# Seven operations per piece of weights, a scale from magnitudes, a convolution planned to end ahead of its transform, and four halves on another engine

## The chip, the cores and the metric

The kernel runs on one core of a Trainium2 chip. A core has a matrix engine (TensorE, PE in the profile), a vector engine (VectorE, DVE), an activation engine (ScalarE, ACT), a general engine (GpSimd, POOL) and a queue for transfers (SyncE, SP). Each works through its own list of instructions in order, and waits on semaphores for the others. The metric is the time of one execution on the device in microseconds (us); the kernel before has a median of 1158.82 us over three runs (1158.05 to 1159.72).

## The reference

Eight batches of 4224 rows with 192 columns go through four steps. The two weight matrices arrive as 64-bit floats, two 32-bit words each.

```python
w = np.exp(weight_gen - max(weight_gen, axis=-1)); w = w / (sum(w) + 1e-09)    # [8, 4224, 8 heads, 7 taps]
x = einsum('bshk,bskhg->bshg', w, windows_of_7_rows(x))      # dynamic convolution, 24 columns to a head
u = x + real(fft(fft(x, axis=1), axis=2))                    # over 4224 rows, then 192 columns
un = (u - mean(u)) / sqrt(var(u) + 1e-06)
out = u + maximum(un @ w_ch1, 0.0) @ w_ch2                   # 192 -> 768 -> 192
```

## The kernel before, in words

**Layout.** 4224 rows are 128 partitions times 33 rows. A batch is worked in nine groups: eight of four rows (128 x 768 elements) and one of a single row. Names carry batch and group: `u_3_0` is batch 3, group 0; in `conv` the first group of a batch is group 0 and the last, of one row, is group 8.

**Convolution** (`conv`, L296). For each group DVE multiplies the rows of `x_sb` by the seven taps (L405; the first product goes into the group's sum `u`, the six others into `pr`, five buffers), and POOL adds them up (L414). Batches 0 and 1 share the sums out otherwise in part. POOL then folds the sum (`sm`, L428), PE makes the first stage of the row transform of it (`pg`, L435), ACT and DVE put that into `gt` (L440 to L446), and SP writes `gt` to a scratch array `g_d` in DRAM (L449). The taps of a batch come from `softmax_taps` (L261): DVE takes the maximum (L273) and subtracts it (L274), ACT the exponential (L276), DVE the sum (L278), the small constant (L279) and the reciprocal (L280), and each group multiplies its own taps by it (L362). From batch 2 on this is one piece of 1848 elements for a batch, and `next_conv` issues it behind the last product of the batch before.

**Transform** (`transform`, L460). SP reads `g_d` back in another order (`g`, L471), PE does the second stage (`pp`, L481), ACT copies it to `pq`. For the first matmul of it the whole convolution of the batch must have gone through `gt`, the write and the read.

**Mix and norm** (`mix`, L502; `norm`, L528). PE does the column transform (`eo`, L510), DVE adds it to `u` (L516 to L525). The norm takes mean and variance on DVE (`bn`, first three groups of batch 0 and first two of batch 1) or on ACT, normalises on ACT (`un`, L565), casts to fp16 (`hl`, L573), and subtracts that from `un` for a second fp16 half in two instructions of 512 and 256 elements (L574, L576). These two are on DVE where `quick` holds, which is for the five groups named, and on POOL elsewhere. SP transposes `hl` into `ht` (L582).

**MLP** (`mlp`, L587). A group has six tiles: PE does the first layer (`ph`, L607, fp16 high and low halves of the weights), ACT takes the positive part into `hh` (L617), DVE its low half (L618), PE the second layer (`po`, L630), DVE scales and adds to `u` (L635), SP writes the group out.

**Weights** (`prep_w1`, `prep_w2`, `split_w2`). The first matrix is unpacked in three pieces before the first MLP, the second in three pieces around it. `words_to_f32` (L194) makes a 32-bit float of the two words of each element in eight DVE instructions of 384 elements, L200 to L212. `weight_scale` (L169) finds a power of two: for each of three pieces it masks the exponent (L176) and takes the maximum (L177), then the maximum over pieces and partitions. `split_f32` makes the fp16 halves, high on ACT (L217), low on DVE (L218).

**Order.** The program is issued as streams, each with a start and an end in units of an MLP group: `add(start, end, gen)`, and `run` takes the stream that is due next. For batch b >= 2, with t0 = 9 b, the transform goes from t0 - 4.4 (`PP_AT`) to t0 - 3.0, and the convolution from `free_at`, where the transform of the batch before was due, to t0 - 4.4. Batch 1 has numbers of its own, and the MLP of batch 0's group 7 is in part held behind its transform. A scheduler then sets the order of each engine from dependencies and its own estimate of durations, so a small change of these numbers moves rows on every engine.

Of the kernel before, what the change touches and what calls it, by code (L numbers as in the profile page):

```python
# [10 lines left out]
F16 = mybir.dt.float16  # L11
F32 = mybir.dt.float32
I32 = mybir.dt.int32
AF = mybir.ActivationFunctionType
ALU = mybir.AluOpType
AX = mybir.AxisListType
# [14 lines left out]
EARLY = 7.4  # L31
HELD = 7.0
SPLIT = 4
PP_AT = 4.4
MIX_STEP = 0.8
PE_SUMS = {(0, 0), (0, 1), (0, 3), (0, 5), (0, 7)}
POOL_TAPS = {(0, 0): (5, 6), (0, 1): (5, 6), (0, 3): (6,), (1, 0): range(7), (1, 1): range(7)}
# [51 lines left out]
def tile_dynconv_fnet_mlp(  # L89
# [76 lines left out]
    def temp(nm, dt):  # L166
        return sb.tile([P, PW], dt, tag="hh", name=nm, bufs=10)

    def weight_scale(words, bits, nm):  # L169

        mask, unit, least, up, down = {32: (0x7F800000, 1.0, 4.0 * 2 ** 23, 257.0, -3.0),
                                       64: (0x7FF00000, 8.0, 900.0 * 2 ** 20, 1153.0, -899.0)}[bits]
        mx = cpool.tile([P, len(words)], F32, name=f"mx_{nm}")
        for i, word in enumerate(words):
            ex = temp(f"ex_{nm}{i}", I32)
            nc.vector.tensor_scalar(out=ex, in0=word, scalar1=mask, scalar2=None, op0=ALU.bitwise_and)  # L176
            nc.vector.tensor_reduce(out=mx[:, i:i + 1], in_=ex, axis=AX.X, op=ALU.max)  # L177
        m1 = cpool.tile([P, 1], F32, name=f"m1_{nm}")
        nc.vector.tensor_reduce(out=m1, in_=mx, axis=AX.X, op=ALU.max)
        m2 = cpool.tile([P, 1], F32, name=f"m2_{nm}")  # L180
        row = pst("ph", 3, [P, P], F32, f"mr_{nm}")
        nc.tensor.matmul(row[0:1, :], lhsT=m1, rhs=ident32, start=True, stop=True)
        nc.vector.tensor_reduce(out=m2[0:1], in_=row[0:1, :], axis=AX.X, op=ALU.max)
        every = pst("ph", 3, [P, 1], F32, f"me_{nm}")
        nc.tensor.matmul(every, lhsT=ones, rhs=m2[0:1], start=True, stop=True)
        nc.vector.tensor_scalar_max(out=m2, in0=every, scalar1=least)
        sc = cpool.tile([P, 2], I32, name=f"sc_{nm}")
        nc.vector.tensor_scalar(out=sc[:, 0:1], in0=m2, scalar1=-unit, scalar2=up * 2 ** 23,
                                op0=ALU.mult, op1=ALU.add)
        nc.vector.tensor_scalar(out=sc[:, 1:2], in0=m2, scalar1=unit, scalar2=down * 2 ** 23,  # L190
                                op0=ALU.mult, op1=ALU.add)
        return sc.bitcast(F32)

    def words_to_f32(raw, out, nm, bank):  # L194

        hi, lo = raw[:, :, 1], raw[:, :, 0]
        v = nc.vector
        a, w = [pst(*bank, [P, PW], dt, f"{x}_{nm}") for x, dt in (("pa", I32), ("pw", F32))]
        t = temp(f"t_{nm}", I32)
        v.tensor_scalar(out=a, in0=hi, scalar1=3, scalar2=0x3FFFFFFF,  # L200
                        op0=ALU.logical_shift_left, op1=ALU.bitwise_and)
        v.scalar_tensor_tensor(out=t, in0=hi, scalar=-0x40000000, in1=a, op0=ALU.bitwise_and, op1=ALU.bitwise_or)
        v.tensor_scalar(out=a, in0=hi, scalar1=0x7FF00000, scalar2=None, op0=ALU.bitwise_and)
        v.scalar_tensor_tensor(out=w, in0=a, scalar=float(0x38100000), in1=t.bitcast(F32),
                               op0=ALU.is_ge, op1=ALU.mult)
        v.tensor_scalar(out=t, in0=w.bitcast(I32), scalar1=23, scalar2=23,
                        op0=ALU.logical_shift_right, op1=ALU.logical_shift_left)
        v.tensor_scalar(out=a, in0=lo, scalar1=3, scalar2=None, op0=ALU.logical_shift_right)
        r = t.bitcast(F32)
        v.scalar_tensor_tensor(out=r, in0=a, scalar=2.0 ** -49, in1=r, op0=ALU.mult, op1=ALU.mult)  # L210
        out = w if out is None else out
        last_word.append(v.tensor_tensor(out=out, in0=w, in1=r, op=ALU.add))  # L212
        return out
# [314 lines left out]
    def norm(b, g):  # L528

        T = min(4, N2 - 4 * g)  # L530
        u = uv = us[b, g]
        st = sb.tile([P, 4, 2], F32, tag="st", name=f"st_{b}_{g}", bufs=2)
        rs = sb.tile([P, 3, 4], F32, tag="rs", name=f"rs_{b}_{g}", bufs=2)
        junk = sb.tile([P, D], F16, tag="junk", name=f"junk_{b}_{g}", bufs=2)
        quick = NG * b + g < QUICK or (b == 1 and g < 2)
        if NG * b + g < QUICK:
            halves = [pst("ph", 3, [P, 2, D], F32, f"un_{b}_{g}_{i}") for i in range(2)]
        else:
            un = sb.tile([P, 4, D], F32, tag="un", name=f"un_{b}_{g}", bufs=1)
            halves = [un[:, 0:2], un[:, 2:4]]  # L540
        if quick:
            bn = sb.tile([P, 4, 6], F32, tag="bn", name=f"bn_{b}_{g}", bufs=2)
            for t in range(T):
                nc.vector.bn_stats(out=bn[:, t, :], in_=uv[:, t, :])
                last_bn[b, g] = nc.vector.bn_aggr(out=st[:, t, :], in_=bn[:, t, :])
            nc.scalar.activation(rs[:, 0, 0:T], st[:, 0:T, 1], AF.Sqrt, bias=eps_t)
            neg = -1.0
        else:
            for t in range(T):
                nc.scalar.activation(junk, uv[:, t, :], AF.Identity, accum_out=st[:, t, 0:1])  # L550
            neg = -1.0 / D
            nc.scalar.mul(rs[:, 2, 0:T], st[:, 0:T, 0], neg)
            for t in range(T):
                nc.scalar.activation(junk, uv[:, t, :], AF.Square, bias=rs[:, 2, t:t + 1],  # L554
                                     accum_out=st[:, t, 1:2])
            nc.scalar.activation(rs[:, 0, 0:T], st[:, 0:T, 1], AF.Sqrt, bias=eps_t, scale=1.0 / D)
        nc.vector.reciprocal(out=rs[:, 0, 0:T], in_=rs[:, 0, 0:T])
        if quick or b == 0:
            for t in range(T):
                nc.vector.tensor_scalar(out=rs[:, 1, t:t + 1], in0=st[:, t, 0:1], scalar1=rs[:, 0, t:t + 1],  # L560
                                        scalar2=neg, op0=ALU.mult, op1=ALU.mult)
        else:
            nc.gpsimd.tensor_tensor(out=rs[:, 1, 0:T], in0=rs[:, 2, 0:T], in1=rs[:, 0, 0:T], op=ALU.mult)  # L563
        for t in range(T):
            nc.scalar.activation(halves[t // 2][:, t % 2, :], uv[:, t, :], AF.Identity,  # L565
                                 bias=rs[:, 1, t:t + 1], scale=rs[:, 0, t:t + 1])
        yield 0.5
        warm = NG * b + g == 0
        hl = sb.tile([P, 4, 2 * D], F16, tag="hl", name=f"hl_{b}_{g}", bufs=2)
        lo_eng = nc.vector if quick else nc.gpsimd  # L570
        spans = [(un, 0, T)] if NG * b + g >= QUICK else [(h, 2 * i, 2 * i + 2) for i, h in enumerate(halves)]
        for src, t0, t1 in spans:
            nc.scalar.copy(hl[:, t0:t1, 0:D], src[:, 0:t1 - t0, :])  # L573
            lo_eng.tensor_tensor(out=hl[:, t0:t1, 2 * P:3 * P], in0=src[:, 0:t1 - t0, 0:P],  # L574
                                 in1=hl[:, t0:t1, 0:P], op=ALU.subtract)
            last_lo[NG * b + g] = lo_eng.tensor_tensor(out=hl[:, t0:t1, D:2 * P], in0=src[:, 0:t1 - t0, P:D],  # L576
                                                       in1=hl[:, t0:t1, P:D], op=ALU.subtract)
        if warm:
            keep_warm(("ph", 3), f"hl{g}", hl[:, 0, 0:P], hl[:, T - 1, 0:2 * D], WARM[2])
        hls[NG * b + g] = hl  # L580
        ht = sb.tile([P, 4, 3, P], F16, tag="ht", name=f"ht_{b}_{g}", bufs=3)
        nc.sync.dma_start(ht[:, 0:T].rearrange("p t q m -> p (t q) m"),  # L582
                          hl[:, 0:T, :].rearrange("p t d -> p (t d)"), transpose=True)
        state[b, g] = (us.pop((b, g)), ht)
        yield 2.0
# [148 lines left out]
    for b in range(B):  # L734
        t0 = NG * b
        pp_at, mix_at, step = (NG - HELD + 0.6, NG - HELD, 0.6) if b == 1 else (PP_AT, 3.0, MIX_STEP)
        if b > 0:
            add(free_at, t0 - pp_at, next_conv(b) if b > 1 else rest())
            add(t0 - pp_at, t0 - mix_at, transform(b))
            free_at = t0 - pp_at  # L740
        for g in range(NG):
            if b > 0 or g >= QUICK:
                at = t0 - mix_at + step * g + (0.7 if b == 0 else 0)
                add(at, at + step, late_mix(g) if b == 0 and g >= QUICK else mix(b, g))
                add(max(at + step, t0 + g - 2.0), t0 + g - 1.0, norm(b, g))
# [38 lines left out]
```

## Time and profile before

| what | value |
|---|---|
| median of three runs | 1158.82 us |
| the profiled execution | 1160.23 us, of which 1158.5 us are the span from the first to the last instruction; 1.73 us lie around it |
| mean granted PE clock | 0.982 |
| busy: PE, DVE, POOL, ACT | 1085.7, 987.3, 873.7, 776.9 us |
| first MLP matmul | at 129.89 us |
| first matmul of the transforms of batches 1 to 7 | 234.72, 360.78, 485.65, 611.49, 738.97, 866.21, 992.99 us |

Times in the trace count from the start of the span. A row of the timeline shows start, duration, engine, line, operation, output and input, how many instructions the row joins, and in square brackets how long the engine was idle before it and what it waited for. The starts of the transforms of successive batches lie 124.87, 125.84, 127.48, 127.24 and 126.78 us apart from batch 2 on. After the last transform has begun 165.5 us are left.

### The profile page before, as it was taken

How to read it: one execution, taken by the hardware profiler on the slowest of the kernel's cores; microseconds unless marked ns; L12 is line 12 of the kernel's file. 1: busy time of each engine (PE TensorE's matmuls, PEld its weight loads, DVE VectorE, ACT ScalarE, POOL GpSimd, SP SyncE). 2: the span in 40 equal slices, each digit the busy share in tenths (PEclk: the TensorE clock that was granted, in tenths of full speed). 3: DMA queues.
4: the chain of work that ended last, by engine and by line, in shares of the span. 5: the costliest groups of instructions: out<-in, count | busy, mean ns of one | idle time of the engine just before them, and what ended most of it. 6: DMA issues, size and time to landing. Idle time of an engine off the chain costs nothing. (4 is left out here: it accounts for less than half of the span.)

```text
span 1158.5 us, 23681 instructions
## 1 busy us (share of the span) xinstructions
PE 1085.7 (94%) x8476; PEld 819.0 (71%) x8476; DVE 987.3 (85%) x1830; ACT 776.9 (67%) x2360; POOL 873.7 (75%) x747
## 2 busy tenths in 40 slices
PE   5787699998799999999999999999999999999998
PEld 3346388776577777678777877778767867777777
DVE  7998998889989998999989998899988997356443
ACT  1014587453896589648985699668974798579832
POOL 5948699699896999699978999599959999011200
PEclk9997799999999999999999999999999999999999
DMA  8325233622474147513564247514652243412321
GB/s 307 118 92 152 41 99 104 183 79 64 122 194 126 52 117 197 142 56 110 131 178 110 59 121 204 137 53 117 160 128 65 56 91 79 126 34 68 83 45 46
DMA packets 156502, 128.72 MB, mean 111 GB/s; under 512 B 108571, under 2 KB 133088, under 8 KB 156384
## 3 DMA queue, kind: packets, MB, share of 16 engines
q1 hardware_dynamic: 156384, 127.21, 40.6%
q8 instruction: 67, 1.10, 0.4%
q14 instruction: 51, 0.42, 0.1%
HBM read 61.46 MB, written 39.37 MB: 87 GB/s over the span
## 5 line engine op out<-in xcount | busy, mean ns | idle before, releaser
L414 POOL TENSOR_TENSOR u<-u,pr 128x768 f32<-128x768 f32 (+1 forms) x395 | 655.7, 1679 | 67.4 <-DVE pr L405 51.5
L630 PEld LDWEIGHTS <-hh 128*128 128x128 f16 x4248 | 364.6, 98 | 81.8 <-DVE hh L618 5.9
L630 PE MATMUL po<-w2h,hh 128*128 128x192 f16 x2832 | 416.2, 246 | 5.6 <-DVE hh L618 4.3
L607 PE MATMUL ph<-ht,w1h 128*128 128x512 f16 (+1 forms) x1296 | 396.2, 363 | 5.9 <-DMA ht<-hl 2.9
L405 DVE TENSOR_TENSOR pr<-x_sb,wp 128x768 f32<-128x768 f32 (+1 forms) x420 | 357.3, 873 | 13.1 <-POOL u L414 10.2
L630 PE MATMUL po<-w2l,hh 128*128 128x192 f16 x1416 | 346.4, 246 | 0.0
L618 DVE SCALAR_TENSOR_TENSOR hh<-ph,hh 128x512 f16<-128x512 f32 (+1 forms) x390 | 244.8, 632 | 110.9 <-ACT hh L617 109.4
L607 PE MATMUL ph<-ht,w1l 128*128 128x512 f16 (+1 forms) x864 | 310.8, 363 | 0.0
L617 ACT ACTIVATE hh<-ph 128x512 f16<-128x512 f32 (+1 forms) x390 | 213.8, 551 | 137.9 <-PE ph L607 110.3
L607 PEld LDWEIGHTS <-w1h 128*128 128x128 f16 x1296 | 125.8, 99 | 92.3 <-issue 2.0
L565 ACT ACTIVATE un<-u,rs 128x192 f32<-128x192 f32 x264 | 123.9, 536 | 23.1 <-POOL rs L563 9.8
L607 PEld LDWEIGHTS <-w1l 128*128 128x128 f16 x864 | 85.1, 98 | 53.9 <-issue 6.6
L574 POOL TENSOR_TENSOR hl<-un,hl 128x512 f16<-128x512 f32 (+1 forms) x67 | 71.8, 1071 | 67.2 <-issue 29.7
L554 ACT ACTIVATE junk<-u,rs 128x192 f16<-128x192 f32 x244 | 110.7, 454 | 3.8
L550 ACT ACTIVATE junk<-u 128x192 f16<-128x192 f32 x244 | 88.1, 361 | 15.6 <-DVE u L520 12.8
L510 PE MATMUL eo<-cs_sb,pq 97*128 97x97 f32 x544 | 82.5, 276 | 5.3 <-DVE u L520 3.7
L485 ACT COPY pq<-pp 97x204 f32<-97x204 f32 (+1 forms) x96 | 46.9, 489 | 55.9 <-PE pp L481 55.8
L510 PEld LDWEIGHTS eo<-cs_sb,pq 97*128 97x128 f32 x544 | 75.2, 193 | 9.9 <-issue 6.7
L635 DVE SCALAR_TENSOR_TENSOR u<-po,isc,u 128x384 f32<-128x384 f32 (+1 forms) x122 | 72.3, 592 | 5.0 <-PE po L630 4.9
L410 PE MATMUL pa<-pr,ident 128*128 128x384 f32 x140 | 53.2, 520 | 21.0 <-POOL pr L403 11.8
L428 POOL TENSOR_TENSOR sm<-u 128x382 f32<-128x382 f32 x64 | 65.5, 1023 | 9.1 <-ACT u L423 8.7
L563 POOL TENSOR_TENSOR rs<-rs 128x4 f32<-128x4 f32 (+1 forms) x61 | 12.1, 200 | 68.3 <-ACT hh L617 38.8
(106 smaller groups left out, 1306.7 us busy)
## 6 DMA issues: line engine op xcount, KB each, us to landing
out_dram<-u SPq DMA_DIRECT2D x64, 384.0 KB
x_sb<-in_x_dram SPq DMA_DIRECT2D x48, 384.0 KB
g<-g_d SPq DMA_DIRECT2D x40, 336.0 KB
x_sb<-in_x_dram SPq DMA_DIRECT2D x8, 864.0 KB
g_d<-gt SPq DMA_DIRECT2D x32, 195.0 KB
g_d<-gt SPq DMA_DIRECT2D x32, 189.0 KB
w<-in_weight_gen_dram SPq DMA_DIRECT2D x6, 924.0 KB
x_sb<-in_x_dram SPq DMA_DIRECT2D x8, 672.0 KB
```

What stands on the lines that cost most here:

```text
L405: last_product[b] = nc.vector.tensor_tensor(out=dst, in0=rows, in1=wk, op=ALU.mult)
L414: adder.tensor_tensor(out=u, in0=u, in1=pr, op=ALU.add)
L510: nc.tensor.matmul(eo[:, e, j, :], lhsT=pq[0:DH, e, r, r:r + P], rhs=cs_sb[:, e, :], start=True, stop=True)
L550: nc.scalar.activation(junk, uv[:, t, :], AF.Identity, accum_out=st[:, t, 0:1])
L554: nc.scalar.activation(junk, uv[:, t, :], AF.Square, bias=rs[:, 2, t:t + 1], accum_out=st[:, t, 1:2])
L565: nc.scalar.activation(halves[t // 2][:, t % 2, :], uv[:, t, :], AF.Identity, bias=rs[:, 1, t:t + 1], scale=rs[:, 0, t:t + 1])
L574: lo_eng.tensor_tensor(out=hl[:, t0:t1, 2 * P:3 * P], in0=src[:, 0:t1 - t0, 0:P], in1=hl[:, t0:t1, 0:P], op=ALU.subtract)
L607: last_ph[n] = nc.tensor.matmul(ph[:, 0:T], lhsT=wt[:, cs_], rhs=ht[:, 0:T, blk], start=(i == 0), stop=(i == len(terms) - 1))
L617: nc.scalar.activation(a[:, 0:T], ph[:, 0:T], AF.Relu)
L618: nc.vector.scalar_tensor_tensor(out=l[:, 0:T], in0=ph[:, 0:T], scalar=0.0, in1=a[:, 0:T], op0=ALU.max, op1=ALU.subtract)
L630: nc.tensor.matmul(po[t // 2][:, t % 2, :], lhsT=hx[:, t], rhs=wx[:, c2, :], start=(c2 == 0 and i == 0), stop=(c2 == NH - 1 and i == len(t ...
L635: nc.vector.scalar_tensor_tensor(out=lt, in0=po[t // 2][:, 0:t % 2 + 1], scalar=scales[0][:, 1:2] if f32 else isc, in1=lt, op0=ALU.mult, o ...
```

## The change

Four things change. `words_to_f32` loses the shift of the lower word (old L208): the lower word is read as an unsigned number straight from the raw words, with a factor of 2 to the power -52 where it was -49, and the exponent goes to `a`, where `t` held it before. `weight_scale` takes the maximum of the magnitude of each piece, read as 32-bit float, and masks the exponent once, of the three maxima. `PP_AT` goes from 4.4 to 4.2 and a new `CONV_LEAD` of 0.2 is taken off the end of a convolution: for batches 2 to 7 the convolution still ends at t0 - 4.4, the transform begins at t0 - 4.2, and the next convolution is due to begin at t0 - 4.2. And the low halves of the first two groups of batch 1 go from DVE to POOL; those of batch 0's first three groups stay on DVE.

```diff
-PP_AT = 4.4
+CONV_LEAD = 0.2
+PP_AT = 4.2
...
         for i, word in enumerate(words):
-            ex = temp(f"ex_{nm}{i}", I32)
-            nc.vector.tensor_scalar(out=ex, in0=word, scalar1=mask, scalar2=None, op0=ALU.bitwise_and)
-            nc.vector.tensor_reduce(out=mx[:, i:i + 1], in_=ex, axis=AX.X, op=ALU.max)
+            nc.vector.tensor_reduce(out=mx[:, i:i + 1], in_=word.bitcast(F32), axis=AX.X, op=ALU.max, apply_absolute_value=True)
+        ex = cpool.tile([P, len(words)], I32, name=f"ex_{nm}")
+        nc.vector.tensor_scalar(out=ex, in0=mx.bitcast(I32), scalar1=mask, scalar2=None, op0=ALU.bitwise_and)
         m1 = cpool.tile([P, 1], F32, name=f"m1_{nm}")
-        nc.vector.tensor_reduce(out=m1, in_=mx, axis=AX.X, op=ALU.max)
+        nc.vector.tensor_reduce(out=m1, in_=ex, axis=AX.X, op=ALU.max)
...
-        v.tensor_scalar(out=t, in0=w.bitcast(I32), scalar1=23, scalar2=23,
+        v.tensor_scalar(out=a, in0=w.bitcast(I32), scalar1=23, scalar2=23,
                         op0=ALU.logical_shift_right, op1=ALU.logical_shift_left)
-        v.tensor_scalar(out=a, in0=lo, scalar1=3, scalar2=None, op0=ALU.logical_shift_right)
         r = t.bitcast(F32)
-        v.scalar_tensor_tensor(out=r, in0=a, scalar=2.0 ** -49, in1=r, op0=ALU.mult, op1=ALU.mult)
+        v.scalar_tensor_tensor(out=r, in0=lo.bitcast(U32), scalar=2.0 ** -52, in1=a.bitcast(F32), op0=ALU.mult, op1=ALU.mult)
...
-        lo_eng = nc.vector if quick else nc.gpsimd
+        lo_eng = nc.vector if NG * b + g < QUICK else nc.gpsimd
...
-            add(free_at, t0 - pp_at, next_conv(b) if b > 1 else rest())
+            add(free_at, t0 - pp_at - (CONV_LEAD if b > 1 else 0), next_conv(b) if b > 1 else rest())
             add(t0 - pp_at, t0 - mix_at, transform(b))
```

The change moves rows on all engines. Three places follow; line numbers of the kernel after are two higher than those of before up to `words_to_f32` and one higher behind it.

DVE at the start of batch 3's convolution, before (`wp_3` its taps, `hh_1_4_3` the low half of MLP tile 3 of batch 1's group 4):

```order
L280 RECIPROCAL wp_3_3463<-wp_3_3463 128x264
L444 TENSOR_TENSOR gt_2_8_3448<-pg_2_8_3446,up_2_8_3450 128x95
L446 TENSOR_TENSOR gt_2_8_3448<-pg_2_8_3446,up_2_8_3450 128x95
L618 SCALAR_TENSOR_TENSOR hh_1_4_2_3400<-ph_1_4_2_3388,hh_1_4_2_3400 128x512
L635 SCALAR_TENSOR_TENSOR u_1_3_1337<-po_1_3_0_3305,isc_88,u_1_3_1337 128x384
L362 TENSOR_TENSOR wp_3_3463<-w_3_3464,wp_3_3463 128x224
L618 SCALAR_TENSOR_TENSOR hh_1_4_3_3443<-ph_1_4_3_3425,hh_1_4_3_3443 128x512
L405 TENSOR_TENSOR u_3_0_3475<-x_sb_66,wp_3_3463 128x768
```

and after:

```order
L281 RECIPROCAL wp_3_3475<-wp_3_3475 128x264
L619 SCALAR_TENSOR_TENSOR hh_1_5_0_3570<-ph_1_5_0_3536,hh_1_5_0_3570 128x512
L619 SCALAR_TENSOR_TENSOR hh_1_5_1_3604<-ph_1_5_1_3596,hh_1_5_1_3604 128x512
L363 TENSOR_TENSOR wp_3_3475<-w_3_3476,wp_3_3475 128x224
L619 SCALAR_TENSOR_TENSOR hh_1_5_2_3643<-ph_1_5_2_3632,hh_1_5_2_3643 128x512
L406 TENSOR_TENSOR u_3_0_3487<-x_sb_66,wp_3_3475 128x768
```

The first product of batch 3 now stands behind tile 2 of group 5, five tiles of the MLP further on. On PE, 25 more matmuls of the first layer and 59 more of the second come ahead of that point, and 24 and 60 more ahead of the first matmul of batch 2's transform. For batches 4, 5, 6 and 7 the first product moves on by two, three, two and one tiles, and the transforms of batches 3 to 7 by 12, 12, 15, 15 and 0 matmuls of the first layer.

DVE at the end of batch 1's convolution, before (`gt_1_8` is the last part that its transform needs):

```order
L446 TENSOR_TENSOR gt_1_6_1790<-pg_1_7_1890,up_1_7_1894 128x2x95
L444 TENSOR_TENSOR gt_1_8_1940<-pg_1_8_1938,up_1_8_1942 128x95
L446 TENSOR_TENSOR gt_1_8_1940<-pg_1_8_1938,up_1_8_1942 128x95
L280 RECIPROCAL wp_2_1956<-wp_2_1956 128x264
L362 TENSOR_TENSOR wp_2_1956<-w_2_1957,wp_2_1956 128x224
L405 TENSOR_TENSOR u_2_0_1968<-x_sb_66,wp_2_1956 128x768
```

and after:

```order
L281 RECIPROCAL wp_2_1942<-wp_2_1942 128x264
L445 TENSOR_TENSOR gt_1_6_1776<-pg_1_7_1876,up_1_7_1880 128x2x95
L447 TENSOR_TENSOR gt_1_6_1776<-pg_1_7_1876,up_1_7_1880 128x2x95
L363 TENSOR_TENSOR wp_2_1942<-w_2_1943,wp_2_1942 128x224
L406 TENSOR_TENSOR u_2_0_1954<-x_sb_66,wp_2_1942 128x768
L406 TENSOR_TENSOR pr_2_0_1_1957<-x_sb_66,wp_2_1942 128x768
L406 TENSOR_TENSOR pr_2_0_2_1993<-x_sb_66,wp_2_1942 128x768
L406 TENSOR_TENSOR pr_2_0_3_2024<-x_sb_66,wp_2_1942 128x768
L406 TENSOR_TENSOR pr_2_0_4_2054<-x_sb_66,wp_2_1942 128x768
L406 TENSOR_TENSOR pr_2_0_5_2084<-x_sb_66,wp_2_1942 128x768
L445 TENSOR_TENSOR gt_1_8_1926<-pg_1_8_1924,up_1_8_1928 128x95
L447 TENSOR_TENSOR gt_1_8_1926<-pg_1_8_1924,up_1_8_1928 128x95
```

The last two parts of `gt_1_8` now stand behind six products of batch 2. Ahead of the first matmul of batch 1's transform PE has 6 more matmuls of the first layer and 7 more of the second.

POOL in batch 2's third group, after (before, the rows are the same without the two of `hl_1_0`):

```order
L429 TENSOR_TENSOR sm_2_2_2476<-u_2_2_2319 128x2x191
L431 TENSOR_TENSOR sm_2_2_2476<-u_2_2_2319 128x2
L415 TENSOR_TENSOR u_2_3_2534<-u_2_3_2534,pr_2_3_3_2568 128x768
L415 TENSOR_TENSOR u_2_3_2534<-u_2_3_2534,pr_2_3_4_2578 128x768
L575 TENSOR_TENSOR hl_1_0_2255<-un_1_0_2209,hl_1_0_2255 128x4x128
L577 TENSOR_TENSOR hl_1_0_2255<-un_1_0_2209,hl_1_0_2255 128x4x64
L415 TENSOR_TENSOR u_2_3_2534<-u_2_3_2534,pr_2_3_5_2600 128x768
```

The two halves of group 0 stand between two adds of batch 2's convolution; those of group 1 between two adds eleven rows on.

1 line of the change is left out of this document (added).

## The prediction

> **What bounds the kernel now.** I read the page's shares of the engines first (PE 94%, DVE 85%, POOL 75%), then a table by batch, then the first matmul of each transform, and from there back to what each waits for. The table has the busy time of PE, its weight loads, DVE, ACT and POOL, with instructions, from one convolution's first add on POOL to the next one's:
>
> ```profile
> 359.06:484.62 125.56, 122.28 (x1040) 93.40 (x1037) 118.46 (x212) 96.36 (x301) 114.00 (x98) 1.00 0.48 127
> 484.62:610.93 126.31, 124.13 (x1054) 95.15 (x1054) 118.43 (x212) 97.65 (x303) 113.92 (x98) 1.00 0.46 124
> 610.93:737.84 126.91, 125.12 (x1064) 96.04 (x1064) 118.54 (x212) 97.86 (x304) 113.96 (x98) 1.00 0.46 121
> 737.84:865.35 127.51, 124.34 (x1060) 95.70 (x1058) 119.14 (x213) 98.77 (x304) 113.85 (x97) 1.00 0.45 115
> 865.35:992.00 126.65, 125.51 (x1050) 95.91 (x1051) 110.27 (x205) 95.38 (x301) 114.00 (x97) 0.99 0.32 81
> ```
>
> PE is busy for 122 to 125.5 us of 125.6 to 127.5, and looks like the bound. But POOL works 114.0 us in every batch, the same to 0.2, and the 11.6 to 13.7 us left over are one gap per batch, in which the taps of the next batch are made in a chain over DVE and ACT. Which of the two ends last is seen where they meet, at the first matmul of each transform (batches 1, 2, 3 and 7), and in the row of what follows it:
>
> ```profile
> 234.72 0.65 PE L481 MATMUL pp<-te_sb,g 102*97 102x102 f32 x5 [1.01 <-DMA g<-g_d]
> 360.78 0.42 PE L481 MATMUL pp<-te_sb,g 102*97 102x102 f32 x2 [1.36 <-DMA g<-g_d]
> 485.65 0.56 PE L481 MATMUL pp<-te_sb,g 102*97 102x102 f32 x4 [2.02 <-DMA g<-g_d]
> 992.99 0.60 PE L481 MATMUL pp<-te_sb,g 102*97 102x102 f32 x5
> 993.00:1158.50 165.50, 162.51 (x1436) 124.47 (x1434) 76.67 (x149) 102.11 (x306) 16.70 (x27) 1.00 0.25 63
> ```
>
> PE waits 1 to 2 us for the convolution, and at batch 7 not at all: the two run neck and neck, the convolution a little behind. After the last transform there are 165.5 us with 162.5 of PE work, which the change leaves alone. So the end moves by as much as 992.99 moves, and that is the later of two arrivals: PE's own, and the chain of convolutions, each begun when the taps are ready and DVE comes to its first product.
>
> **The change part by part.** First the weights: by line, DVE's groups from 70 to 131 us, then the masks of the second matrix (204 to 212), and PE's first MLP matmul:
>
> ```profile
> L208 DVE TENSOR_SCALAR pa_w<-raw_w 128x384 int32<-128x384 int32 x5 | 2.7, 545 | 0.0
> L218 DVE SCALAR_TENSOR_TENSOR w1l<-pw_w,sc_w,w1h 128x384 f16<-128x384 f32 x3 | 1.8, 614 | 5.3 <-ACT w1h L217 5.3
> L176 DVE TENSOR_SCALAR ex_w<-raw_w 128x384 int32<-128x384 int32 x3 | 0.9, 352 | 0.0
> L176 DVE TENSOR_SCALAR ex_w<-w2f 128x384 int32<-128x384 int32 x3 | 2.7, 942 | 0.0
> 129.89 0.39 PE L607 MATMUL ph<-ht,w1h 128*128 128x512 f16 x1 [0.71 <-DMA ht<-hl]
> ```
>
> Three masks go (0.9 us) and one of three columns comes, at most another 0.35; five shifts go (2.7), three of them ahead of the last low half. That is 3.3 us less on DVE at most. But DVE also waits 5.3 us for ACT's high halves there, which can swallow part of it. Between 1.0 and 3.3 I take 1.9, what lies ahead of the waits less a little. The unsigned read and the reduction of magnitudes have no row of before; they replace instructions of the same 384 elements, and I cost them as those: nothing added, at worst half a microsecond for the six that come earlier. The first MLP matmul is then at 128.0. The masks of the second matrix take 2.7 us, of which one of 0.35 at most comes back, and the taps of batch 2 are made right behind them: their first product comes some 2.3 us earlier.
>
> That product matters for batch 1's transform, because the last parts of `gt` now stand behind it and five more. The rows of before on DVE and SP:
>
> ```profile
> 226.71 0.24 DVE L446 TENSOR_TENSOR gt<-pg,up 128x95 f32<-128x95 f32 x1
> 229.14 0.95 DVE L405 TENSOR_TENSOR u<-x_sb,wp 128x768 f32<-128x768 f32 x1
> 230.01 4.40 DVE L405 TENSOR_TENSOR pr<-x_sb,wp 128x768 f32<-128x768 f32 x5
> 227.97 0.57 SPq L450 DMA_DIRECT2D g_d<-gt  x1
> 230.95 1.38 SPq L471 DMA_DIRECT2D g<-g_d  x3
> ```
>
> Before, `gt` was whole at 226.95, its write was issued at 227.97, the read at 230.95, and PE had data at 234.72: 7.8 us. After, the first product is at about 226.9, six products take 5.3, the two parts of `gt` 0.4, so `gt` is whole at 232.6. With the queue free by then the rest takes some 7.2, and data is there at 239.8. PE, with 6 and 7 more matmuls ahead (1.9 us) and its start 1.9 earlier, comes at about 233.7 to 234.5. It waits some 5.4 us, where it waited 1.0: a loss of 4.4.
>
> Next the four halves. Where batch 0 ends, DVE has no idle time; by ten microseconds, then DVE's halves and POOL's adds beside the first, and what halves take on POOL in a later batch:
>
> ```profile
> 270.00:280.00 10.00, 7.08 (x81) 6.48 (x79) 10.00 (x22) 2.76 (x8) 9.07 (x8) 0.99 0.39 90
> 280.00:290.00 10.00, 9.28 (x47) 4.92 (x47) 10.00 (x23) 4.20 (x14) 8.87 (x5) 0.84 0.18 45
> 290.00:300.00 10.00, 6.29 (x43) 5.03 (x42) 10.00 (x18) 9.71 (x38) 8.77 (x8) 0.85 0.37 131
> 300.00:310.00 10.00, 7.57 (x59) 5.51 (x57) 10.00 (x18) 6.75 (x23) 7.96 (x8) 0.98 0.36 79
> 310.00:320.00 10.00, 8.65 (x63) 5.72 (x62) 10.00 (x20) 9.26 (x32) 9.92 (x10) 1.00 0.68 160
> 273.23 1.31 DVE L574 TENSOR_TENSOR hl<-un,hl 128x512 f16<-128x512 f32 x1
> 274.46 2.03 DVE L576 TENSOR_TENSOR hl<-un,hl 128x256 f16<-128x256 f32 x1
> 298.58 1.71 DVE L574 TENSOR_TENSOR hl<-un,hl 128x512 f16<-128x512 f32 x1
> 300.21 2.02 DVE L576 TENSOR_TENSOR hl<-un,hl 128x256 f16<-128x256 f32 x1
> 270.29 7.87 POOL L414 TENSOR_TENSOR u<-u,pr 128x768 f32<-128x768 f32 x4
> L574 POOL TENSOR_TENSOR hl<-un,hl 128x512 f16<-128x512 f32 x8 | 9.2, 1148 | 4.1 <-ACT gt L440 4.1
> L576 POOL TENSOR_TENSOR hl<-un,hl 128x256 f16<-128x256 f32 x8 | 5.3, 662 | 0.0
> ```
>
> DVE loses 7.07 us of work where it is full, and PE idles 11.1 us and runs at a clock of 0.84 and 0.85 for twenty (3.1 us lost). I give PE the 7.07 and half of the clock, 1.5. POOL takes on 2 x (1.15 + 0.66) = 3.6, and has 5.3 us of idle time between 270 and 310 that hides it; without that cover batch 2's convolution would end 3.6 later.
>
> So far PE stands at 1.9 + 7.1 + 1.5 - 4.4 = **6.1 us** ahead at 355. Now the planner's numbers. In front of batch 3's first product stand 25 more first-layer and 59 more second-layer matmuls. The rows around the tile behind which it stood before, on PE, ACT and DVE:
>
> ```profile
> 354.74 0.38 PE L607 MATMUL ph<-ht,w1l 128*128 128x512 f16 x1
> 354.96 0.25 PE L630 MATMUL po<-w2h,hh 128*128 128x192 f16 x1
> 355.12 0.33 PE L630 MATMUL po<-w2h,hh 128*128 128x192 f16 x2
> 355.29 0.25 PE L630 MATMUL po<-w2l,hh 128*128 128x192 f16 x1
> 354.99 0.55 ACT L565 ACTIVATE un<-u,rs 128x192 f32<-128x192 f32 x1 [1.20 <-POOL hl L576]
> 355.82 1.08 ACT L617 ACTIVATE hh<-ph 128x512 f16<-128x512 f32 x2
> 356.57 0.68 DVE L618 SCALAR_TENSOR_TENSOR hh<-ph,hh 128x512 f16<-128x512 f32 x1
> 357.17 0.94 DVE L405 TENSOR_TENSOR u<-x_sb,wp 128x768 f32<-128x768 f32 x1
> ```
>
> Starts are 0.22 us apart in the first layer and 0.085 in the second: 25 x 0.22 + 59 x 0.085 = 10.5 us of PE work. Of this 1.0 was slack, since ACT came to that tile 1 us after PE had done it. The first product moves by 10.5 - 1.0 - 6.1 = **+3.4 us**. Queued behind it on DVE are the other products, and POOL waits for these.
>
> From there the chain of convolutions runs by itself. PE reaches the transform of batch 3 at 485.65 - 2.02 = 483.6 before; after, it comes 6.1 earlier with 12 matmuls of the first layer and 29 of the second more (5.1 us), while the convolution is 3.4 later. The tiles that the taps' chain is threaded between are then long done. The five periods show what that may be worth: the shortest is 125.56, the next three are 0.75, 1.35 and 1.95 longer and the fifth (to 992) 1.09, with POOL's work unchanged. I take all of it back, **-5.1**; it can be anything from 0 to that, as POOL's queue, not PE, holds part of the chain.
>
> Sum: +3.4 - 5.1 = -1.7. The profiled execution of 1160.23 would be 1158.5, and the median, 1.41 below it, **1157.1 us**.
>
> **The rivals.** *The gate does not bind.* Nothing shows that batch 1's later `gt` costs PE all of 4.4, and PE's idle time at the end of batch 0 may go altogether: 1.9 + 11.1 + 1.5 = 14.5 us, more than 9.5. Then batch 3 starts as early as its taps allow, 1.9 sooner, and with the 5.1 the end is 7.0 earlier, 1151.8. For it speaks that DVE is at 10.00 for fifty microseconds, against it the row of `gt` behind six products.
>
> *The gate costs more than is won back* (slower). Batch 1's mix and norm hang on the late transform, so DVE's freed time is in part spent waiting for it: 3.5 of 7.07, and PE comes out of its long wait at a clock of 0.84, which cost 1.6 us in the row at 280. PE then stands at 1.9 + 3.5 - 4.4 - 1.6 = -0.6 at 355, batch 3's first product is at +10.1, and even with 5.1 back the end is 5.0 later: 1163.8. It decides once PE is less than 2.1 us ahead there, since 9.5 - 2.1 - 5.1 = 2.3. [...]
>
> *The halves only move the collision.* DVE's halves end at 274.54 and 276.49, each 0.3 us behind the end of one of POOL's adds (every 1.97 from 270.29: 274.22, 276.19), and the 256 elements take longer than the 512: DVE was held while POOL worked. With the halves on POOL, DVE may be held for them in turn, at most their 3.6 us. PE is then 2.5 ahead, the product at +7.0, the end at +1.9: 1160.7, no change that can be told. [...]
>
> **How the numbers follow.** A measurement of this kernel can tell about 0.2%, 2.3 us, from no change. Forecast: 0.45 (its own range 1153.5 to 1162, as the 5.1 may be less and the 6.1 more), of which 0.22 faster, 0.21 within, 0.02 slower. Gate not binding: 0.23, all faster. Gate costs more: 0.22, of which 0.20 slower. Halves collide: 0.10, of which 0.08 within and 0.02 slower. Together 0.45, 0.31 and 0.24. The range from 1150 to 1163.5 takes in most of both outer cases.
>
> **What would show it.** First MLP matmul near 128.0, not 129.9. The first matmul of batch 1's transform near 239.8 with 5 us of waiting; at 235 the 4.4 falls. No halves on DVE at 270 to 300 and PE busy for 9 or more of each ten there. Batch 3's first product near 360.6, right behind a tile; at 355 the first rival holds, past 364 the second. PE waiting 7 us or more for batch 3's data. And the periods from batch 3 on at 125.6: if they stay at 126 to 127.5, the -5.1 is wrong and the kernel is slower.

## The result, and the profile after

The kernel after takes 1169.01 us (median of 4 runs, 1168.46 to 1170.07), the kernel before beside it 1159.27 us (1158.05 to 1160.41): a ratio of 1.0085, interval 1.0068 to 1.0103. It is slower by 9.7 us, where 1.7 us faster was forecast and 1163.5 was the upper end. The profiled execution has a span of 1167.6 us, 9.1 more than before.

PE's timeline of the kernel after, the first MLP matmul and the first matmul of the transforms of batches 1, 2, 3, 5 and 7:

```profile
125.56 0.39 PE L608 MATMUL ph<-ht,w1h 128*128 128x512 f16 x1 [1.29 <-DMA ht<-hl]
240.50 1.65 PE L482 MATMUL pp<-te_sb,g 102*97 102x102 f32 x8 [5.44 <-DVE u L636]
365.32 0.91 PE L482 MATMUL pp<-te_sb,g 102*97 102x102 f32 x8 [0.81 <-DMA g<-g_d]
491.60 0.94 PE L482 MATMUL pp<-te_sb,g 102*97 102x102 f32 x8 [1.13 <-DMA g<-g_d]
751.19 0.91 PE L482 MATMUL pp<-te_sb,g 102*97 102x102 f32 x8 [1.41 <-DMA g<-g_d]
1000.22 1.03 PE L482 MATMUL pp<-te_sb,g 102*97 102x102 f32 x8 [1.98 <-DMA g<-g_d]
```

The MLP starts 4.3 us earlier and the first transform behind it 5.8 later, after the wait of 5.4 us that the prediction had. (The row puts this wait down to a DVE instruction that ended just before; in a kernel below whose order is the same here, e3, the same wait ends on the read of `g`.) Batches 2 and 3 are 4.5 and 5.9 us late, batch 5 is 12.2, batch 7 is 7.2. The last 1.9 come behind it, where PE's clock is 0.83 over ten microseconds after its wait of 2.0.

POOL's timeline, the first adds of batches 2 and 3, and then the table by ten microseconds (PE, its loads, DVE, ACT, POOL, granted clock) at batch 1's transform and where batch 2's MLP begins:

```profile
230.79 9.38 POOL L415 TENSOR_TENSOR u<-u,pr 128x768 f32<-128x768 f32 x5 [13.93 <-DVE pr L406]
362.43 13.12 POOL L415 TENSOR_TENSOR u<-u,pr 128x768 f32<-128x768 f32 x7 [5.25 <-DVE pr L406]
```

```profile
230.00:240.00 10.00, 5.06 (x28) 3.56 (x26) 9.93 (x15) 1.19 (x2) 8.89 (x5) 0.99 0.36 99
240.00:250.00 10.00, 9.50 (x54) 9.36 (x55) 6.37 (x8) 5.96 (x16) 10.00 (x8) 0.50 0.53 151
...
280.00:290.00 10.00, 7.62 (x58) 5.03 (x55) 10.00 (x25) 4.66 (x15) 9.53 (x7) 1.00 0.31 79
290.00:300.00 10.00, 8.08 (x62) 5.81 (x61) 10.00 (x20) 9.41 (x39) 9.04 (x7) 1.00 0.66 178
...
410.00:420.00 10.00, 4.61 (x44) 3.39 (x42) 10.00 (x24) 8.32 (x37) 10.00 (x10) 0.86 0.43 100
420.00:430.00 10.00, 10.00 (x51) 5.62 (x50) 8.71 (x16) 9.57 (x32) 10.00 (x9) 0.80 0.50 152
```

Batch 2's first add is only 0.24 us earlier than before, though the MLP began 4.3 us earlier: POOL's gap in front of it has grown from 10.2 to 13.9 us. PE idles 5 us at 230 to 240 and then runs at half its clock for ten. Where batch 0 ends (280 to 300) PE does better than before. But where batch 2's MLP begins there is a new hole of 5.4 us, with a clock of 0.86 and 0.80 in the ten microseconds that hold it and the next ten. Half of it is one wait, which the rows of PE and of the transposing transfer show (the rest are waits for DVE, 2.1 us for low halves `hh` and 0.6 for the mix):

```profile
419.63 0.59 PE L608 MATMUL ph<-ht,w1h 128*128 128x512 f16 x1 [2.69 <-DMA ht<-hl]
```

```profile
415.60 1.48 SPq L583 DMA_TRANSPOSE ht<-hl  x1
```

The transfer is issued 50.3 us after batch 2's transform began, and PE comes for its data 51.6 us after (at 419.63 less the 2.69 of waiting). Before, it was issued at 409.45, 48.7 us behind the transform, and PE had 24 first-layer and some 60 second-layer matmuls more to do in between.

DVE's timeline in front of batch 2's convolution, after:

```profile
208.92 5.08 DVE L258 TENSOR_TENSOR isc<-sc_w,sc_w 128x1 f32<-128x1 f32 x1
213.93 1.70 DVE L219 SCALAR_TENSOR_TENSOR w2l<-w2f,sc_w,w2h 128x384 f16<-128x384 f32 x2
...
228.90 0.95 DVE L406 TENSOR_TENSOR u<-x_sb,wp 128x768 f32<-128x768 f32 x1
```

and POOL's beside it:

```profile
207.79 5.23 POOL L415 TENSOR_TENSOR u<-u,pr 128x192 f32<-128x192 f32 x5
212.97 1.01 POOL L429 TENSOR_TENSOR sm<-u 128x382 f32<-128x382 f32 x1
213.92 0.21 POOL L431 TENSOR_TENSOR sm<-u 128x2 f32<-128x2 f32 x1
```

An instruction on one column took 5.08 us, to 214.00. In that time POOL went through five instructions without a pause, four adds (the first already running) and the fold of 1.01 us, with which it ended; POOL went on behind it. Before, the same one took 0.44 us at 220.44, near the end of POOL's run there. With the weights' edits the whole split of the second matrix (scale, high and low halves) came ahead of batch 1's last product, and so from POOL's gap into POOL's busy stretch.

### The profile page after: what moved, and what is told of

Same layout as the page of the kernel before. It is cut to its first block, busy times and chain, and to the rows that moved or that the text cites. A ratio compares the mean times of both kernels' runs of the same rounds, so it can differ in the third digit from the quotient of the medians.

```text
span 1167.6 us, 23637 instructions
## 1 busy us (share of the span) xinstructions
PE 1091.3 (93%) x8476; PEld 825.0 (71%) x8476; DVE 983.4 (84%) x1816; ACT 779.0 (67%) x2360; POOL 875.5 (75%) x751
## 4 chain that ended last, share of the span: by engine, by line
PE 49%; DVE 19%; ACT 9%; DMA 8%; POOL 8%; issue 7%; SPq 0%; DVEq 0%; POOLq 0%; ACTq 0%
PE ph L608 19%; PE po L631 17%; DVE pr L406 8%; PE pp L482 5%; POOL u L415 5%; DMA ht<-hl 3%; PE pa L411 3%; PE eo L511 2%; DMA g<-g_d 2%; DVE hh L619 2%; DMA g_d<-gt 2%; PE pg L436 2%; ACT junk L555 2%; ACT hh L618 2%; ACT junk L551 1%
## 5 line engine op out<-in xcount | busy, mean ns | idle before, releaser
L406 DVE TENSOR_TENSOR pr<-x_sb,wp 128x768 f32<-128x768 f32 (+1 forms) x420 | 361.6, 883 | 16.5 <-POOL u L415 13.1
L619 DVE SCALAR_TENSOR_TENSOR hh<-ph,hh 128x512 f16<-128x512 f32 (+1 forms) x390 | 247.5, 642 | 114.2 <-ACT hh L618 113.1
L575 POOL TENSOR_TENSOR hl<-un,hl 128x512 f16<-128x512 f32 (+1 forms) x69 | 74.4, 1079 | 68.0 <-ACT hl L574 31.0
L631 PE MATMUL po<-w2f,hh 128*128 128x192 f32 x336 | 63.0, 327 | 2.6 <-DVE u L636 1.4
```

What stands on the lines that cost most here:

```text
L406: last_product[b] = nc.vector.tensor_tensor(out=dst, in0=rows, in1=wk, op=ALU.mult)
L619: nc.vector.scalar_tensor_tensor(out=l[:, 0:T], in0=ph[:, 0:T], scalar=0.0, in1=a[:, 0:T], op0=ALU.max, op1=ALU.subtract)
L631: nc.tensor.matmul(po[t // 2][:, t % 2, :], lhsT=hx[:, t], rhs=wx[:, c2, :], start=(c2 == 0 and i == 0), stop=(c2 == NH - 1 and i == len(t ...
```

## The experiments

**First four: each part alone, and the change without the halves.** The edits are those of the diff above, one part at a time: only the two numbers; only

```diff
-        lo_eng = nc.vector if quick else nc.gpsimd
+        lo_eng = nc.vector if NG * b + g < QUICK else nc.gpsimd
```

on the kernel before; only `weight_scale` and `words_to_f32`; and the kernel after with that one line put back.

> Only the planner's numbers (PP_AT 4.2, CONV_LEAD 0.2) on the kernel before. Theory A (the halves on POOL make the scheduler put batch 2's transform so late that its first norm has no cover): here 115 first-layer matmuls stand between batch 2's transform and its first MLP, as before, so the time stays within 3 us of before (1156 to 1162) and PE has no hole of 2 us or more where batch 2's MLP begins. Theory B (the planner's numbers move the transforms, as the prediction had it): slower by 5 us or more, 1164 and up. Theory C (the late last part of gt of batch 1 from the weights' edits): no change, first matmul of batch 1's transform near 234.7.

> Only the four halves go to POOL. Theory A: 95 first-layer matmuls are left between batch 2's transform and its first MLP where 115 were; slower by 6 to 10 us (1165 to 1169), PE idle for 4 us or more and then at a low clock where batch 2's MLP begins. Theory B: DVE relieved of 7 us, 1153 to 1159. Theory C: no change, batch 1's transform near 234.7.

> Only the unpacking in seven operations and the scale from magnitudes. First MLP matmul 3 to 4 us earlier than 129.9. Theory A: batch 2's transform stands 125 first-layer matmuls ahead of its MLP, no hole there; 1153 to 1160. Theory B: 1155 to 1159. Theory C: the last part of gt of batch 1 stands behind products of batch 2, first matmul of its transform near 240 after a wait of 5 us; slower by 3 us or more.

> The whole change but the halves, which stay on DVE. Theory A: 125 first-layer matmuls between batch 2's transform and its first MLP, no hole; 1153 to 1160. Theory B: 1163 to 1170, as the planner's numbers are in it. Theory C: 1162 and up, with batch 1's transform near 240.

| kernel | median, us | ratio to before | interval |
|---|---|---|---|
| numbers only (e1) | 1152.58 | 0.9954 | 0.9939 to 0.9970 |
| halves only (e2) | 1161.01 | 1.0033 | 1.0014 to 1.0052 |
| weights only (e3) | 1173.37 | 1.0132 | 1.0116 to 1.0148 |
| all but the halves (e4) | 1175.70 | 1.0152 | 1.0132 to 1.0172 |

Theory B, the prediction's own picture of the numbers, falls: they make the kernel faster, and the move of batch 2's transform that the prediction laid to them is not theirs. With the numbers alone 115 first-layer matmuls stand between batch 2's transform and its first MLP, as before; with the halves alone 95, with both and the weights 91. It is the halves that move it. But the 6 to 10 us that theory A gave the halves alone do not come: e2 takes 0.3% more than the kernel before, and its waits where batch 2's MLP begins are 1.8 and 1.2 us. The weights' edits cost most, and the wait at batch 1's transform comes with them, as theory C had it. In e3:

```profile
239.92 1.65 PE L481 MATMUL pp<-te_sb,g 102*97 102x102 f32 x8 [5.00 <-DMA g<-g_d]
```

But the halves make the rest faster (1175.7 to 1169.0), so no one part explains the 9.7 us.

**The held instruction.** Three kernels with one instruction in another form; every engine's order is as it was, row by row.

```diff
-        nc.vector.tensor_tensor(out=isc, in0=scales[0][:, 1:2], in1=s2[:, 1:2], op=ALU.mult)
+        nc.vector.tensor_scalar(out=isc, in0=scales[0][:, 1:2], scalar1=s2[:, 1:2], scalar2=None, op0=ALU.mult)
```

> The kernel after with one instruction in another form: the product of the two scales (isc, L258, one column) reads one of them as a scalar operand, so it has one tensor input from memory where it had two; every engine's order is the same. Theory D (that instruction is held for 5.08 us by POOL's adds, since the weights' edits moved it from POOL's gap into POOL's busy stretch): it takes 0.15 us, batch 2's first product comes near 224 to 226 where it was at 228.9, batch 1's transform near 235 to 237 where it was at 240.5, and the time falls by 4 to 7 us from 1169.0, to 1162 to 1165. Theory C (only the place of gt of batch 1 behind six products costs): batch 1's transform stays past 239 and the time within 2 us of 1169. Theory A (the short way from batch 2's transform to its MLP): the hole of PE at 410 to 420 stays or grows whatever happens to the rest.

> The weights' edits alone with the same form of the one instruction. Theory D: falls from 1173.4 by 5 us or more, to 1160 to 1168; batch 1's transform 4 to 5 us earlier than 239.9. Theory C: stays within 2 us of 1173.

> Weights' edits and planner's numbers, halves on DVE, the same form of the one instruction. Theory D: falls from 1175.7 by 5 us or more, to 1163 to 1170. Theory C: within 2 us of 1175.

Measured: 1169.77 (ratio 1.0109, 1.0089 to 1.0130), 1174.37 (1.0144, 1.0114 to 1.0174) and 1175.63 us (1.0160, 1.0135 to 1.0184). Nothing was won, and theory D in this form falls. DVE's timeline of e5 says why:

```profile
208.78 0.21 DVE L258 TENSOR_SCALAR isc<-sc_w,sc_w 128x1 f32<-128x1 f32 x1
209.37 5.93 DVE L219 SCALAR_TENSOR_TENSOR w2l<-w2f,sc_w,w2h 128x384 f16<-128x384 f32 x2 [0.37 <-ACT w2h L218]
```

The instruction with one tensor input takes 0.21 us, and the next with two is held in its place: two low halves take 5.93 us where three took 1.67 before. In the change, e3 and e4 (5.06 to 5.08 us) as in e5 and e6 (5.93 and 5.92 for two) it is the first instruction with two inputs from SBUF that is held while POOL works without a break. The products were not held: of the change's 485 the longest took 0.98 us, and their second input, the taps, lies in PSUM. That the place of the inputs decides is not shown, as no run moves one. Nor does a rule for the length of a hold follow from the five instructions of POOL over which the change's went: in e14, one of the last runs below, DVE and POOL have the same instructions in the same order up to this place, and DVE gets in after 1.24 us (in the change five of POOL's adds take 5.23 there, 1.05 each):

```profile
209.46 1.24 DVE L257 TENSOR_TENSOR isc<-sc_w,sc_w 128x1 f32<-128x1 f32 x1
210.62 3.11 DVE L218 SCALAR_TENSOR_TENSOR w2l<-w2f,sc_w,w2h 128x384 f16<-128x384 f32 x2
```

Batch 2's first product then comes at 227.07, 1.8 us before that of the change. So the long hold itself is worth some 2 us (an estimate from these two executions), and why it falls out long or short is open.

**gt ahead of the products, with the split left where the change put it.** As e5, and

```diff
-        yield from behind(last_product[b - 1].ins, conv(b))
+        yield from behind(last_gt[1].ins if b == 2 else last_product[b - 1].ins, conv(b))
```

> As e5, and batch 2's convolution is issued behind the last part of gt of batch 1, so that this part stands ahead of the six products again. The scheduler then leaves 70 first-layer matmuls between batch 2's transform and its MLP, where e5 has 91. Theory C: batch 1's transform without a wait over 1.5 us, and 3 us or more faster than e5. Theory A: PE's hole where batch 2's MLP begins grows to 8 us or more, and it is slower than e5.

1171.56 us (1.0122, 1.0100 to 1.0145), not to be told from e5. Batch 1's transform comes at 231.95 without a wait, and the gain is lost again: PE's waits where batch 2's MLP begins are

```profile
409.90 0.89 PE L436 MATMUL pg<-sm,f_sb 128*128 128x192 f32 x4 [2.08 <-DVE u L521]
414.01 1.99 PE L511 MATMUL eo<-cs_sb,pq 97*128 97x97 f32 x8 [3.22 <-DVE u L521]
420.62 0.58 PE L608 MATMUL ph<-ht,w1h 128*128 128x512 f16 x1 [4.61 <-DMA ht<-hl]
```

9.9 us. With 70 first-layer matmuls between batch 2's transform and its MLP, theory A holds for the hole. Theory C, by which the late `gt` alone costs, did not get its 3 us; but the run does not refute it, for its edit costs something of its own. The taps of batch 2 are now made behind `gt`, and batch 2's first product, at 228.90 in the change, stands at

```profile
236.46 0.95 DVE L406 TENSOR_TENSOR u<-x_sb,wp 128x768 f32<-128x768 f32 x1
```

What the run shows is the price of the late `gt` at batch 1's transform: 8.2 us there (240.16 in e5).

**The split put back.** The kernel after, the same with the halves on DVE, and the weights' edits alone, each with

```diff
         with tc.issue_after(last_ph[SPLIT].ins):
-            queue(last_product[1].ins, (split_w2, None))
+            queue(last_gt[1].ins, (split_w2, None))
```

after which the split stands behind the taps' subtraction, and `gt` ahead of batch 2's first product, as before the change.

> The kernel after, with the second matrix's split issued behind the last part of gt of batch 1, where it stood before: the scales' product and the three low halves (w2l) come in POOL's gap again, behind the taps' subtraction, and gt of batch 1 stands ahead of batch 2's products. Theory F (the weights' edits cost by moving the split into POOL's busy stretch, where the first instruction with two tensor inputs from memory is held for 5 us, the scales' product or the low halves alike, and by putting gt behind the products): the held instruction is gone (0.4 and 1.7 us), batch 1's transform comes at 229 to 232 with a wait under 2 us, batch 2's first product at 224 to 226, and the time falls to 1153 to 1162. Theory A (the 95 matmuls between batch 2's transform and its MLP, from the halves on POOL): it does not fall below 1163, with a hole of 5 us at the start of batch 2's MLP.

> As e9 with the halves on DVE: weights' edits and planner's numbers. Theory F: falls by 12 us or more from the 1175.7 of the same without the split held back, to 1150 to 1160. If instead the weights' edits cost through the order of batches 2 to 6 (125 and more matmuls between transform and MLP, PE waiting for each convolution), it stays above 1165.

> Weights' edits alone, with the split held back. Theory F: 1153 to 1162, 11 us or more below the 1173.4 without it. If the cost is the order of batches 2 to 6: above 1165.

| kernel | median, us | ratio to before | interval |
|---|---|---|---|
| the change, split put back (e9) | 1150.21 | 0.9921 | 0.9897 to 0.9946 |
| the same, halves on DVE (e10) | 1170.33 | 1.0102 | 1.0066 to 1.0137 |
| weights only, split put back (e11) | 1168.26 | 1.0091 | 1.0060 to 1.0122 |

e9 beats both kernels. By one line of order it is 7.4 us faster than the kernel before beside it, where the change was 9.7 slower: 17.1 us between them. Its rows on DVE and PE:

```profile
213.69 0.45 DVE L258 TENSOR_TENSOR isc<-sc_w,sc_w 128x1 f32<-128x1 f32 x1
217.33 1.67 DVE L219 SCALAR_TENSOR_TENSOR w2l<-w2f,sc_w,w2h 128x384 f16<-128x384 f32 x3
221.65 0.24 DVE L447 TENSOR_TENSOR gt<-pg,up 128x95 f32<-128x95 f32 x1
222.23 0.95 DVE L406 TENSOR_TENSOR u<-x_sb,wp 128x768 f32<-128x768 f32 x1
```

```profile
228.09 0.91 PE L482 MATMUL pp<-te_sb,g 102*97 102x102 f32 x8 [0.59 <-DMA g<-g_d]
353.03 0.94 PE L482 MATMUL pp<-te_sb,g 102*97 102x102 f32 x8 [0.64 <-DMA g<-g_d]
```

Nothing is held, batch 2's first product comes 6.7 us earlier than in the change, batch 1's transform 12.4, batch 2's 12.3. Theory F holds for the change, and the times came out below its ranges. The line undoes three things at once and does not tell their shares apart: the hold, the `gt` behind the products, and the split ahead of the taps' subtraction. For e10 and e11 theory F does not hold: they fall by 5 us and stay above 1165, as the rival named beside it had it (the order of batches 2 to 6). Without the halves on POOL, part of an earlier start is lost where batch 0 ends, some 3 us (the table below); the rest goes from batch 3 on. DVE's halves in e10, and PE there by ten microseconds:

```profile
268.55 2.17 DVE L575 TENSOR_TENSOR hl<-un,hl 128x512 f16<-128x512 f32 x1
270.65 2.02 DVE L577 TENSOR_TENSOR hl<-un,hl 128x256 f16<-128x256 f32 x1
292.81 2.00 DVE L575 TENSOR_TENSOR hl<-un,hl 128x512 f16<-128x512 f32 x1
294.73 2.02 DVE L577 TENSOR_TENSOR hl<-un,hl 128x256 f16<-128x256 f32 x1
```

```profile
270.00:280.00 10.00, 4.75 (x26) 2.37 (x24) 10.00 (x20) 1.22 (x3) 7.03 (x7) 0.74 0.38 79
290.00:300.00 10.00, 4.96 (x28) 4.25 (x28) 10.00 (x18) 6.86 (x32) 7.59 (x6) 0.59 0.30 72
```

The halves are the same kind of instruction, two inputs from SBUF, and take 8.2 us in all, those of 256 elements 2.02 each and those of 512 2.00 and 2.17, where an add of POOL beside the old halves took 1.97; PE loses half of each of these stretches and runs at 0.74 and 0.59.

**Which edit of the weights, and the numbers in company.** Only `words_to_f32`; only `weight_scale`; the change with the old numbers, with the split put back and without.

> Only the unpacking in seven operations; the scale is made as before. The split of the second matrix and the last part of gt of batch 1 keep their places (behind the taps' subtraction; ahead of batch 2's first product). Theory F: low halves not held (1.7 us for three), batch 1's transform without a wait over 1.5 us, 1153 to 1162. Theory G (with the halves on DVE, an earlier start is lost again where batch 0 ends, because the scheduler moves batch 2's transform ahead to 125 first-layer matmuls from its MLP): 1163 to 1170, like the 1168 of the weights' edits with the split held back.

> Only the scale from magnitudes; eight operations as before. The split stands behind the last product of batch 1, ahead of the taps' subtraction; gt stays ahead of batch 2's products. Theory F: the low halves are held for at most 2 us; batch 1's transform without a long wait; 1153 to 1164. Theory G: 1163 to 1170.

> Weights' edits, halves on POOL and the split held back, with the planner's numbers of before. If the numbers matter, it is 3 us or more slower than the 1150.2 of the same with the new numbers; if the place of the split and the halves are all, 1148 to 1153.

> The change without the planner's numbers. Theory F: the split is in POOL's busy stretch here too, so it is within 4 us of the change, 1165 to 1173. If the numbers are what costs: below 1160.

Measured: 1170.49 (1.0118, 1.0083 to 1.0154), 1172.60 (1.0127, 1.0109 to 1.0145), 1152.86 (0.9961, 0.9941 to 0.9980) and 1162.18 us (1.0045, 1.0028 to 1.0063). Neither edit of the weights alone moves the split ahead of the last product; it takes both. Yet each alone is slow with the halves on DVE, above theory F's range and at or above the end of theory G's. Theory G's place fits e12, which loses 3.8 us between the transforms of batches 1 and 2; it does not fit e15, which loses 0.2 there and is 4.7 behind already at batch 1's, after PE waited 4.2 us for DVE in batch 1's convolution. The numbers: beside the split put back, the old ones give 1152.9 against 1150.2, within the 1148 to 1153 given for "the place of the split and the halves are all", and the two intervals touch; a gain is not shown. Without it they cost 4.9 us, each against the kernel before beside it, and e14 falls between the ranges of both its theories.

**All of them in one table.** PE's lag behind the kernel before, at the first matmul of the transforms of batches 1, 2 and 3 and at the end of the span: the difference in time, less what the order puts in front of it (by the distance of starts in the traces 0.2165 us for a first-layer matmul, 0.0833 for a second-layer one, 0.326 for one of the first batch's in f32, which the trace has as two rows of 0.163). "Way" is the number of first-layer matmuls between batch 2's transform and its MLP. Each row is one profiled execution; the medians of e2, e9, e11 and e13 lie some 3 us above theirs and that of e12 6 below, so differences of 2 or 3 us mean little.

| kernel | halves on | split | way | batch 1 | batch 2 | batch 3 | end |
|---|---|---|---|---|---|---|---|
| the change | POOL | early | 91 | +2.2 | -5.7 | +0.9 | +9.1 |
| e5 | POOL | early | 91 | +1.9 | -3.4 | +3.1 | +9.4 |
| e14 | POOL | early | 91 | +0.3 | -5.0 | +1.2 | +2.3 |
| e8 | POOL | early, gt first | 70 | -5.5 | -9.7 | +4.6 | +12.4 |
| e2 | POOL | as before | 95 | -0.6 | -8.3 | -6.1 | -2.4 |
| e9 | POOL | put back | 95 | -7.0 | -16.4 | -16.0 | -12.9 |
| e13 | POOL | put back | 95 | -5.6 | -15.4 | -11.4 | -10.3 |
| e1 | DVE | as before | 115 | -2.0 | -2.1 | -4.4 | -8.0 |
| e12 | DVE | as before | 125 | +0.5 | +4.3 | +6.7 | +16.3 |
| e15 | DVE | behind the product | 120 | +4.7 | +4.9 | +5.8 | +11.1 |
| e3 | DVE | early | 125 | +1.6 | +5.3 | +6.2 | +13.4 |
| e4 | DVE | early | 125 | +2.3 | +6.0 | +7.6 | +13.1 |
| e6 | DVE | early | 125 | +2.8 | +6.2 | +7.6 | +12.9 |
| e7 | DVE | early | 125 | +3.5 | +7.2 | +8.9 | +14.4 |
| e10 | DVE | put back | 125 | -5.7 | -2.3 | -1.1 | +9.5 |
| e11 | DVE | put back | 125 | -5.9 | -3.0 | -2.9 | +4.6 |

Four things are read off. From the start to batch 1, an early split with both edits is 7.5 to 9.2 us worse than one put back (e3 against e11, the change against e9). From batch 1 to batch 2, every kernel with the halves on POOL gains 4 to 10 us, and none with them on DVE gains more than 0.1. From batch 2 to batch 3, what is lost goes with the way: 14.3 us at 70, 6.2 to 6.6 at 91, 0.4 to 4.0 at 95, and between a gain of 2.3 and a loss of 2.4 from 115 on. That the way is the cause is argued and not shown: among the kernels with the halves on POOL every way under 95 goes with an early split, and in e14, with the same 91, the wait in this place is another (3.4 us for a fold of POOL). And from batch 3 to the end the change loses 8.2 us, more than in any stretch ahead of it, and e5 and e8 lose 6.3 and 7.8; e14, with the old numbers, loses 1.1. In the change 5.1 of the 8.2 lie between the transforms of batches 4 and 5, where PE waits again for a transposing transfer and its clock falls twice (0.90 from 620 to 630, 0.83 from 690 to 700):

```profile
689.11 0.38 PE L608 MATMUL ph<-ht,w1h 128*128 128x512 f16 x1 [1.99 <-DMA ht<-hl]
```

What the kernels with the weights' edits and the halves on DVE lose from batch 3 on, 5 to 11 us, comes piecemeal and is not settled; nor is what e9 does differently from e13 in batch 2, with the same way.

## Why the prediction was wrong, by its steps

**The start** was mis-sized: the MLP began 4.3 us earlier, not 1.9. Each edit alone gives 1.0 and 1.4 us (e12 and e15, at 128.91 and 128.45), both together 3.4 to 5.7 in the twelve kernels that have them. Part of this may be scatter, for e1, which leaves the weights alone, starts at 127.47. The waits for ACT that could "swallow part of it" shrank instead, from 5.3 to 3.1 us.

**Batch 2's first product** was put at 226.9 and came at 228.90. The masks were gone, but the split was held by POOL for 5 us. This is the first step that failed to the slow side. The prediction had the halves on DVE held by POOL's adds, with rows, and called it a rival for the halves only; it did not ask which other instruction with two inputs the order had moved into POOL's busy stretch. In e14, where the hold was short, it comes at 227.07, as forecast. With the split put back it comes at 222.23, so the edits were worth 6.9 us there, three times the 2.3.

**Batch 1's late gt** was right in size, 5.44 us of waiting against 5.4, at 240.50 against 239.8, and in part by luck: `gt` was whole 1.9 us later than forecast (234.50 against 232.6), and its way through write and read took 6.0 us where 7.2 were given. The 7 second-layer matmuls in front were costed at 0.085 us each; they are f32 ones of 0.326, 1.7 us more. The low clock behind it (0.50 for ten microseconds) stood only in the slower rival, at 1.6.

**The halves** were right: PE gains 7.9 us between batches 1 and 2 against 7.1 + 1.5, and without them (e4) it loses 3.7.

**PE's lead at 355** and **batch 3's first product** were right: 5.7 ahead at batch 2's transform against 6.1, and POOL's first add 3.4 us later against +3.4. The first was luck in part: the start gave 2.4 us more than forecast, and on the way to batch 1's transform PE lost 6.5 where 4.4 were given. The cause was named wrongly: the halves, not the planner's numbers, move batch 2's transform (e1 and e2).

**The -5.1** is the term of the sum that failed. The four periods from batch 3's first add to batch 7's were to shrink to 125.56 each; they grew from 506.3 to 512.4 us in all: 129.06, 126.90, 130.83 and 125.64. So the step that failed is "from there the chain of convolutions runs by itself" with PE ahead of it. The chain did not: in the first of these periods POOL is idle for 15.1 us where it was 11.6, and in the third for 16.9 where it was 13.0. In the first, one wait is new,

```profile
408.10 5.38 POOL L415 TENSOR_TENSOR u<-u,pr 128x768 f32<-128x768 f32 x3 [2.20 <-DVE pr L406]
```

for a product that DVE does behind the additions of batch 2's mix (L517 to L521). Nor did PE stay ahead: its 5.7 us at batch 2's transform are a lag of 0.9 at batch 3's, lost in the hole at 410 and the low clock behind it (0.86 and 0.80). The prediction had PE wait 7 us or more for batch 3's data, and it waited 1.1. It followed the transform's later place only forward to the next convolution, and not to what is between it and its own batch's MLP, the mix, the norm and the transposing transfer, whose places in the plan had not moved. That way had shrunk from 115 matmuls to 91, as the order shows, and it was not counted. What lengthens the third period, and with it the loss behind batch 3, stays open.

**The rivals.** The slower one had the sign and, at 1163.8, about half of the size; its place (batch 1's mix and norm, PE less than 2.1 us ahead at 355) is refuted, since PE was 5.7 ahead. "The gate does not bind" describes e9: there, once the split is put back, PE is 16.4 us ahead at batch 2. "The halves only move the collision" falls: POOL's halves took 1.16 and 0.67 us, and PE gained nearly all that was hoped for. (Its reading of the old halves was off by little: they end 0.55 and 0.28 us behind adds that end at 273.99 and 276.21.)

## What to carry to other kernels

A transform, a load or any hand-over that is moved later takes its time from what follows it in the same batch as much as it gives to what comes ahead: count the work between it and its first reader, in the order itself, before anything else. When an edit shortens one engine's chain, look at what the scheduler then pulls forward, and check each pulled instruction against what the neighbour engine does at that time. Here edits that each look local were worth between -0.5% and +1.5%, alone and in company, by the order that they induced, and one line that put a pulled-forward step back was worth 1.6%.

## What was not expected of the hardware

A DVE instruction on a single column with two inputs from SBUF was held for 5.06 to 5.08 us in three kernels (the change, e3, e4) over five instructions of POOL, and got through as a fold ended, though POOL went on without a pause. In e14, with the same order on both engines, it got through in 1.24 us, and where POOL is idle it takes 0.16 (e12). So the length of such a hold could not have been read from the order. Products whose second input lies in PSUM took 0.94 us beside adds of 1.8 (medians of the kernel before). And PE's clock was granted at 0.50 for the ten microseconds behind a wait of 5.4 us, though PE was busy for 9.5 of them.
